# SyncE steps that a build-time planner holds back, and fifteen weight low parts moved to GpSimd

## The chip, the cores and the metric

The kernel runs on one core of a Trainium2 chip. The metric is the device time of one execution in microseconds (us); lower is better. One core has TensorE (PE in the profile: matmuls and transposes, reading its operands from SBUF and writing PSUM), VectorE (DVE), ScalarE (ACT), GpSimd (POOL) and SyncE (SP), which here only starts DMA transfers. Every engine executes its instructions in the order in which the program holds them, and SP and ACT each start their DMAs in that order too.

## What is computed

The reference is one transformer block over x of 2048 tokens by 640, in fp32: a pre-norm sliding-window attention with 32 heads of 20 and a window of 256 keys, an output projection and the residual, then a pre-norm GEGLU feed-forward with 1536 inner columns and a second residual.

```python
q, k, v = split(layernorm(x) @ wqkv)              # 32 heads of 20
scores = q @ k.T * 20 ** -0.5                     # key j visible to query i if 0 <= i - j < 256
h = x + softmax(masked scores) @ v @ wo
out = h + (gelu(layernorm(h) @ w_gate) * (layernorm(h) @ w_up)) @ w_down
```

## The kernel before

**Tiles.** The tokens are 16 blocks of 128; two blocks make a chunk (8 chunks of 256 tokens). The 640 columns are 5 slices of 128 (`KC` = 5). The feed-forward is cut in three column groups of 512 (`FG` = 3). A product in fp32 precision is made as three fp16 matmuls: each operand is split into a high part, its fp16 value, and a low part, the fp16 value of what is left, and hi·hi, hi·lo and lo·hi are added up in PSUM. So each weight matrix needs a high and a low part (`w3h` and `w3l` are those of the output projection wo; the tile `gu` holds those of the first gate and up groups).

**Weights.** The class `Weight` loads a matrix in 5 slices (128 x 640, or 128 x 512 for gate and up) through a ring `wsl` of three slots, once for the largest value and once more for the split. `split` makes the high part on ScalarE (scale, round to fp16) and then queues `low`, which makes the low part in one of two ways: VectorE reads the fp32 slice, scales it and subtracts the high part in one `scalar_tensor_tensor`; or, for the first `spread` slices, ScalarE scales the fp32 slice in place and GpSimd subtracts. Before, `SPREAD` is 0, and gate and up's first group gave no number: all their low parts are VectorE's. When the low part is done, the slot of the ring is free again.

**Attention.** For each block, `x_lane` loads x into `xt`, normalises it, makes its two fp16 parts (`xp`) and turns them with two DMA transposes, `xh<-xp` and `xl<-xp`. The products of a chunk for q and k go through ScalarE and VectorE to DRAM (`qk<-qks`, started on ACT's queue). The generator `stack` then brings them back in another layout: twelve loads on SP for each chunk, six `qT<-qk` and six `kT<-qk` of 160 KB each. It waits until q or k of the chunk is written, and until block 2c-3 has made its scores, since the new k overwrites keys in the ring `kT` that this block was the last to read. For each pair of heads of a block TensorE then makes scores in one form to find row maxima (`maxima`; VectorE reads them, `junk`), and in the other form for the exponents (`scores`; ScalarE's `pt<-rb,esc`), GpSimd masks the exponents in place (`pt<-pt`), and TensorE multiplies them with v (`pv<-pt,v`). The rows `rb` and `ra` are the two PSUM tiles for scores: the first `rb<-kT,qT` of a chunk is the first matmul that needs its loads. After the output projection VectorE adds the residual, which `residual` loads on SP (`ht<-in_x_dram`), and `wo_out` stores the sum on SP (`h_dram<-ht`).

**Feed-forward.** It starts near 500 us in the span, beside attention at first. Here `ht<-h_dram` brings the sums back, and weight sums (`ws`, `wsums`) are made on VectorE and GpSimd and exchanged through DRAM. The maxima `am` of later weights come from VectorE too.

**What sets the order.** The program is written by a planner, run when the kernel is built. Each piece of work is a generator that yields before each step the engines it needs (`self.engs`) and a function `self.need()`, the planner's time at which its operands will be there. The class `Clock` keeps a planned time for each engine from fixed durations. The main loop walks the lanes in order of rank; the first whose `Lane.start(now)` holds is stepped and writes its instructions. So the order within each queue is fixed at build time, and on the chip nothing passes an instruction ahead of it. Steps with TensorE among their engines have a rule of their own; for all others the last lines of `start` decide:

```python
return (all(nc.t[e] <= now + back for e in self.engs if e != "sync")
        and self.need() <= now + 0.1)
```

A step that only starts a DMA on SP has `self.engs == ("sync",)`: the first line is empty for it, and it is written as soon as the planned time is within 0.1 us of its operands' arrival. Where a DMA stands in SP's queue and its operands come later on the chip than planned, all behind it waits.

All device work goes through a recording helper, so nearly every row of the profile has its line, L199; the tile names tell the rows apart.

Of the kernel before, what the change touches and what calls it, by code (L numbers as in the profile page):

```python
# [24 lines left out]
KC = D // P  # L25
# [228 lines left out]
def block_kernel(ctx: ExitStack, tc: tile.TileContext, x, wqkv, wo, wg, wu, wd, out):  # L254
# [27 lines left out]
    def done(name):  # L282
# [12 lines left out]
    NW, AHEADQ = 3, 6  # L295
    SPREAD = 0
# [5 lines left out]
    FFBACK = dict(split_lane=0.4, scale_lane=0.4, chunk_lane=0.3, token_sums=0.1,  # L302
                  sums_lane=0.2, norm_lane=0.2)
    EARLY = 0.6
    PACE = 1.0
    SWAY = 4

# [12 lines left out]
    def on(eng, *reads, when=None, after=None):  # L320
        f = need(*reads, when=when, eng=eng)
        if after is not None:
            return (eng,), lambda: max(f(), nc.others(after, eng))
        return (eng,), f
# [214 lines left out]
    def products(n, term, ready=None, at_=None):  # L539


        ps = [at_[0]] if at_ else []
        col = at_[1] if at_ else 0

        def start(i):
            if ready and not ready(i) or not ps and opened["mm"] >= banks["mm"]:
                return INF
            t = nc.ready([x for ab in term(i) for x in ab], "tensor")
            return t if ps else max(t, nc.slot(psums["mm"], "mm", banks["mm"]))

        for i in range(n):
            yield ("tensor",), lambda i=i: start(i)
            if not ps:
                ps.append(bank("mm"))
            m = term(i)
            for k, (l, r) in enumerate(m):
                if k:
                    yield pe()
                o = ps[0][:, col:col + r.free_size()]
                nc.tensor.matmul(o, l, r, start=(i == 0 and k == 0),  # L560
                                 stop=(i == n - 1 and k == len(m) - 1))
                pos["dense"] += r.free_size() * 3 // len(m)
        return o
# [19 lines left out]
    wq = wqp.enter_context(tc.tile_pool(name="wq", bufs=1, side="right"))  # L583
    wp = attn.enter_context(tc.tile_pool(name="wp", bufs=1))
# [3 lines left out]
    gu = ffw.tile([P, 4 * KC * 512], F16, name="gu")  # L588
# [3 lines left out]
    gu = gu.rearrange("p (a c f) -> p a c f", c=KC, f=512)  # L592
# [174 lines left out]
    def stack(c, which, d):  # L767
# [10 lines left out]
        for par in range(2):  # L778
            for m, i in enumerate(((0, 0, 1), (0, 1, 0))[which]):
                rows = slice(64 * par + DH * m, 64 * par + DH * m + DH)  # L780
                if c > 1:
                    yield ("sync",), lambda: nc.moved["sync"] - PACE
                nc.sync.dma_start(to[rows], d.rearrange("(a d i) m n -> a m d i n", a=2,
# [652 lines left out]
    def split_lane():  # L1436
        for i, w in [(1, weights[1]), (0, weights[0]), *enumerate(weights)][:2] + list(
                enumerate(weights))[2:]:
            yield on("scalar", when=lambda: w.scaled)
            if i <= NW:  # L1440
                yield from w.split(wq if i < NW else wp, SPREAD)
                continue
            yield on("scalar", when=lambda: W["v"].ready)
            kind, fg = later[i - NW - 1]
            if fg == 0 and kind != "d":
                a = 2 * (kind == "u")
                yield from w.split((gu[:, a], gu[:, a + 1]))
                continue
            k = 1 if fg else 0
            yield on("scalar", when=lambda: ffpools[k])  # L1450
            yield from w.split(ffpools[k], 2)
# [106 lines left out]
    class Lane:  # L1558
# [11 lines left out]
        def start(self, now):  # L1570

            if "tensor" in self.engs:
                return nc.t["tensor"] <= now + AHEAD and self.need() <= max(now, nc.t["tensor"])
            name = self.gen.__name__
            back = self.back
            if name in ("split_lane", "scale_lane"):
                back = PREP if not W["o", 0].ready else FFPREP
            elif name == "x_lane":
                back = EARLY if not B[XF].full else LATE
            elif name == "max_out" and not W["v"].ready:  # L1580
                back = RAMPMAX
            if isinstance(self.engs, Soon):
                back = max(back, OUT)
            if ffpools[1]:
                back = FFBACK.get(name, OUT)
            return (all(nc.t[e] <= now + back for e in self.engs if e != "sync")
                    and self.need() <= now + 0.1)

    load_x(0)
    load_x(1)  # L1590
# [3 lines left out]
    for i, n in enumerate("qkv"):  # L1594
        W[n].load(rooms[n])
        W[n].room(wq)
        if i:
            load_x(i + 1)
    load_x(NR)
    lanes = [x_lane([0], "x"), x_lane([1], "xb"), x_lane([2], "xc"), x_lane([3], "xd"),  # L1600
             x_lane(range(NR, NB), "x"),
             split_lane(), *(scale_lane([i], str(i)) for i in range(NW)),
             scale_lane(range(NW, len(weights)), "0"), load_lane(), ones_lane(), big_lane(),
             first_norm_lane()]
# [6 lines left out]
    now = 0.0  # L1611
# [85 lines left out]
```

## Time and profile before

| | before |
|---|---|
| time, median of 3 runs | 1022.89 us (1022.6 to 1025.46) |
| the profiled execution, its own time | 1022.7 us |
| its span | 1020.8 us |
| TensorE clock granted, mean over the span | 0.998 |
| TensorE busy | 998.5 us (98%) |
| VectorE busy | 748.3 us (73%) |
| ScalarE busy | 437.9 us (43%) |
| GpSimd busy | 299.4 us (29%) |

The span runs from the first to the last instruction of the profiled execution; its own time holds 1.9 us more. A row of the busy table gives for an engine the time in which it worked, its share of the span and the number of instructions. A row of the waits gives the waiting engine and tile, what released it, and then the total in us, the number of times and the longest. A row of the timeline gives a start, a duration, engine, operation, the tile written `<-` the tiles read, a count where like rows are joined, and in brackets the idle time before it with its releaser. Rows with SPq show when SP started a DMA, not when it landed.

### The profile page before, as it was taken

The page shows a single profiled execution, that of the slowest core. Times are in us where ns is not written, and L with a number is a line of the kernel's source. Part 1 is how long each engine was busy: PE and PEld are TensorE (multiplying, and loading weights), DVE is VectorE, ACT ScalarE, POOL GpSimd, SP SyncE. Part 2 cuts the span into 40 slices and gives each one's busy share as a digit, 9 for nine tenths or more (in the row PEclk, how much of TensorE's full clock was granted, in tenths as well). Part 3 has the DMA queues.
Part 4 walks back from the last instruction along what each step waited for, and adds up shares of the span by engine and source line. Part 5 has one row for each costly group of instructions (what it writes and reads, how often), then busy time and mean ns, then how long its engine had stood idle before and what let it go on. Part 6 is the DMA issues. An engine that isn't in the chain of part 4 may idle for free.

```text
span 1020.8 us, 30772 instructions
## 1 busy us (share of the span) xinstructions
PE 998.5 (98%) x12925; PEld 698.8 (68%) x12925; DVE 748.3 (73%) x2221; ACT 437.9 (43%) x706; POOL 299.4 (29%) x489
## 2 busy tenths in 40 slices
PE   8999999998999999999999999989999999999998
PEld 7876677675776766776655664567777777777776
DVE  6888999885776757675688787798996975544553
ACT  6514645664445654555557643522222222221220
POOL 7102224343333432333335511254313300000000
PEclk9999999999999999999999999999999999999999
DMA  8658686271460723315303433233553532222211
GB/s 306 135 116 172 190 167 169 75 132 55 95 140 20 121 75 85 75 45 106 131 29 105 84 126 103 78 129 106 154 181 90 162 137 78 78 97 85 78 53 52
DMA packets 105835, 112.68 MB, mean 110 GB/s; under 512 B 38368, under 2 KB 79584, under 8 KB 105696
## 3 DMA queue, kind: packets, MB, share of 16 engines
q1 hardware_dynamic: 93600, 99.97, 36.4%
q10 hardware_dynamic: 12096, 10.75, 3.4%
q8 instruction: 101, 1.65, 0.7%
q14 instruction: 38, 0.31, 0.1%
HBM read 73.73 MB, written 28.84 MB: 100 GB/s over the span
## 4 chain that ended last, share of the span: by engine, by line
PE 83%; DMA 7%; DVE 5%; issue 2%; ACT 2%; SPq 1%; POOL 0%; DVEq 0%; ACTq 0%; POOLq 0%
PE mm L199 43%; PE pv L199 12%; PE ra L199 12%; PE rb L199 10%; PE tp L199 7%; DMA kT<-qk 3%; DMA qk<-qks 2%; DVE junk L199 1%; SPq L199 1%; DMA qT<-qk 1%; ACT pt L199 1%; DVE am L199 0%; DVE w1l L199 0%; DVE ht L199 0%; DMA wsl<-in_wo_dram 0%
## 5 line engine op out<-in xcount | busy, mean ns | idle before, releaser
L199 POOL TENSOR_SCALAR_AFFINE_SELECT pt<-pt 128x512 f32<-128x512 f32 x352 | 176.7, 518 | 277.5 <-ACT pt L199 261.4
L199 DVE CUSTOM_DVE_ANT_0 junk<-rb,band 128x320 bf16<-128x320 f32 x224 | 109.5, 489 | 48.5 <-PE rb L199 43.3
L199 DVE CUSTOM_DVE_ANT_0 junk<-ra,band 128x320 bf16<-128x320 f32 x224 | 109.4, 489 | 38.9 <-PE ra L199 33.4
L199 ACT ACTIVATE pt<-rb,esc 128x640 f32<-128x640 f32 (+2 forms) x129 | 98.3, 769 | 81.2 <-PE rb L199 65.5
L199 ACT ACTIVATE pt<-ra,esc 128x640 f32<-128x640 f32 (+2 forms) x127 | 96.6, 767 | 75.0 <-PE ra L199 63.9
L199 PE MATMUL pv<-pt,v 128*21 128x128 f32 x2880 | 105.3, 276 | 0.3 <-POOL pt L199 0.2
L199 PEld LDWEIGHTS <-ah 128*128 128x128 f16 x768 | 75.1, 98 | 28.4 <-issue 1.2
L199 ACT ACTIVATE gel<-gel,ffk 128x512 f32<-128x512 f32 x36 | 26.0, 722 | 144.0 <-DVE gel L199 144.0
L199 PEld LDWEIGHTS pv<-pt,v 128*21 128x21 f32 x2880 | 68.8, 100 | 10.8 <-issue 1.0
L199 PEld LDWEIGHTS <-ws 128*128 128x128 f16 x720 | 70.4, 98 | 8.2
L199 PEld LDWEIGHTS <-qT 60*64 60x64 f16 x1280 | 30.4, 104 | 66.4 <-issue 53.1
L199 PEld LDWEIGHTS <-kT 62*64 62x64 f16 x2880 | 63.5, 107 | 11.6 <-issue 8.0
L199 PEld LDWEIGHTS <-gu 128*128 128x128 f16 x440 | 42.0, 98 | 36.1 <-issue 1.7
L199 DVE SCALAR_TENSOR_TENSOR ht<-mm,ffk,ht 128x320 f32<-128x320 f32 x96 | 52.2, 545 | 12.0 <-PE mm L199 10.0
L199 ACT CAST ah<-gel 128x512 f16<-128x512 f32 x48 | 29.7, 618 | 66.7 <-DVE gel L199 64.7
L199 PE MATMUL mm<-xh,w1h 128*128 128x256 f16 x200 | 54.7, 274 | 0.9 <-DVE qks L199 0.9
L199 PE MATMUL mm<-xl,w1h 128*128 128x256 f16 x200 | 54.7, 273 | 0.0
L199 PE MATMUL mm<-xh,w1l 128*128 128x256 f16 x200 | 54.7, 273 | 0.0
L199 PE MATMUL rb<-kT,qT 60*64 60x320 f16 (+4 forms) x636 | 41.2, 283 | 9.5 <-DMA kT<-qk 8.8
L199 PE MATMUL mm<-w3h,oh 128*128 128x320 f16 x160 | 48.2, 301 | 0.0
L199 PE MATMUL mm<-w3l,oh 128*128 128x320 f16 x160 | 48.2, 301 | 0.0
L199 PE MATMUL mm<-w3h,ol 128*128 128x320 f16 x160 | 48.2, 301 | 0.0
(299 smaller groups left out, 2522.5 us busy)
## 6 DMA issues: line engine op xcount, KB each, us to landing
ws<-wsums SPq DMA_DIRECT2D x24, 640.0 KB
qk<-qks ACTq DMA_DIRECT2D x32, 256.0 KB
qT<-qk SPq DMA_DIRECT2D x48, 160.0 KB
kT<-qk SPq DMA_DIRECT2D x48, 160.0 KB
wsums<-ws SPq DMA_DIRECT2D x12, 640.0 KB
ht<-in_x_dram SPq DMA_DIRECT2D x16, 320.0 KB
h_dram<-ht SPq DMA_DIRECT2D x16, 320.0 KB
ht<-h_dram SPq DMA_DIRECT2D x16, 320.0 KB
```

Source lines behind the costliest of these rows:

```text
L199: r = real(*args, **kw)
```

## The change

Two rules of the planner change. First, a step that only starts a DMA on SP is written when its operands have, by the planner's clock, been there for 1 us (`HELD`), where before it could be written 0.1 us ahead of them. The loads of q and k (`stack`) and the weights' loads (`load_lane`) keep the old rule. Held are the stores `h_dram<-ht`, the residual's loads `ht<-in_x_dram`, the loads of x (`xt`), the turns `xh<-xp` and `xl<-xp`, and the feed-forward's exchanges through DRAM (`wsl` and `ht` from `h_dram`, the turns of h, `wsums` and `ws`). Second, all five low parts of wo and all five of each of the first gate and up groups take the second way: ScalarE scales the slice in place, GpSimd subtracts.

```diff
     EARLY = 0.6
+    HELD = 1.0
     PACE = 1.0
...
             if i <= NW:
-                yield from w.split(wq if i < NW else wp, SPREAD)
+                yield from w.split(wq if i < NW else wp, SPREAD if i < NW else KC)
                 continue
...
             if fg == 0 and kind != "d":
                 a = 2 * (kind == "u")
-                yield from w.split((gu[:, a], gu[:, a + 1]))
+                yield from w.split((gu[:, a], gu[:, a + 1]), KC)
                 continue
...
                 back = max(back, OUT)
             if ffpools[1]:
                 back = FFBACK.get(name, OUT)
+            late = 0.1 if self.engs != ("sync",) or name in ("stack", "load_lane") else -HELD
             return (all(nc.t[e] <= now + back for e in self.engs if e != "sync")
-                    and self.need() <= now + 0.1)
+                    and self.need() <= now + late)
```

Every matmul stays; SP has as many instructions as before. The order moves on all engines from about 84 us of the span on, and TensorE's is the same again from about 680 us. Three places are shown.

SP's queue around the loads of chunk 3, before (`qk_2547` and `qk_2930` are chunk 3's q and k in DRAM; the turns and loads of x among them belong to later blocks):

```order
L199 DMA qT<-qk_2547 20x16x256 x5
L199 DMA ht<-in_x_dram 128x640
L199 DMA_TRANSPOSE xh<-xp 128x5x128
L199 DMA_TRANSPOSE xl<-xp 128x5x128
L199 DMA xt<-in_x_dram 128x640
L199 DMA qT<-qk_2547 20x16x256
L199 DMA kT<-qk_2930 20x16x256 x5
L199 DMA_TRANSPOSE xh<-xp 128x5x128
L199 DMA_TRANSPOSE xl<-xp 128x5x128
L199 DMA xt<-in_x_dram 128x640
L199 DMA kT<-qk_2930 20x16x256
```

The same place of the change, where the same data are called `qk_2566` and `qk_3073`:

```order
L199 DMA ht<-in_x_dram 128x640
L199 DMA qT<-qk_2566 20x16x256 x6
L199 DMA kT<-qk_3073 20x16x256 x6
L199 DMA h_dram<-ht 128x640
L199 DMA ht<-in_x_dram 128x640
L199 DMA_TRANSPOSE xh<-xp 128x5x128
```

The twelve loads now follow each other; the four turns and two loads of x that stood among them stand elsewhere.

SP's queue around the loads of chunks 6 and 7, the last two, before:

```order
L199 DMA qT<-qk_7165 20x16x256 x6
L199 DMA kT<-qk_7788 20x16x256 x6
L199 DMA h_dram<-ht 128x640
L199 DMA ht<-in_x_dram 128x640
L199 DMA h_dram<-ht 128x640
L199 DMA qT<-qk_8927 20x16x256 x3
L199 DMA ht<-in_x_dram 128x640
L199 DMA qT<-qk_8927 20x16x256 x3
L199 DMA kT<-qk_9349 20x16x256 x6
```

And in the change:

```order
L199 DMA qT<-qk_7585 20x16x256 x6
L199 DMA kT<-qk_7946 20x16x256 x3
L199 DMA h_dram<-ht 128x640
L199 DMA kT<-qk_7946 20x16x256 x3
L199 DMA ht<-in_x_dram 128x640
L199 DMA h_dram<-ht 128x640
L199 DMA ht<-in_x_dram 128x640
L199 DMA h_dram<-ht 128x640
L199 DMA ht<-in_x_dram 128x640
L199 DMA qT<-qk_9219 20x16x256 x6
L199 DMA kT<-qk_9903 20x16x256 x3
L199 DMA h_dram<-ht 128x640
```

In both chunks a store of a residual sum now stands between the third and the fourth load of k; the last three loads of chunk 7 follow behind the last row shown.

GpSimd's queue at the first gate and up weights, in the change (`AFFINE_SELECT pt<-pt` are the masks, `gu<-wsl,gu` the subtractions; the rows `lyx` and `lyh` belong to layer norms):

```order
L199 TENSOR_TENSOR lyh<-lveh,mhalf 128x1
L199 TENSOR_TENSOR gu<-wsl,gu 128x512 x2
L199 AFFINE_SELECT pt<-pt 128x4x64 x2
L199 AFFINE_SELECT pt<-pt 128x4x128
L199 TENSOR_TENSOR gu<-wsl,gu 128x512
L199 AFFINE_SELECT pt<-pt 128x4x64 x2
L199 AFFINE_SELECT pt<-pt 128x4x128
L199 TENSOR_TENSOR gu<-wsl,gu 128x512
```

Before, only masks and rows of layer norms stood here: subtractions of 512 or 640 columns now stand between the masks of one pair of heads and the next, one or two at a time.

## The prediction, made before the changed kernel had run

> **What bounds the kernel now.** I read the busy table first, then TensorE's waits, then the places in the timeline where the long waits end, then who was late there.
>
> ```profile
> PE 998.5 (98%) x12925; PEld 698.8 (68%) x12925; DVE 748.3 (73%) x2221; ACT 437.9 (43%) x706; POOL 299.4 (29%) x489
> ...
> PE rb L199 <- DMA kT<-qk: 8.8, 4, 4.7
> ...
> PE tp L199 <- DVE am L199: 1.9, 1, 1.9
> ...
> PE mm L199 <- DVE ht L199: 0.4, 1, 0.4
> ...
> PE pv L199 <- POOL pt L199: 0.2, 1, 0.2
> ```
>
> TensorE works in 998.5 of 1020.8 us. The change leaves its matmuls as they are, so it can win only out of the 22.3 us in which TensorE stands, and the rest of its waits are small or lie ahead of the first row that moves. The largest is one thing: four times, 8.8 us in all, the first scores of a chunk wait for the loads of k. The other candidate is VectorE in the feed-forward, 1.9 and 0.4 us. GpSimd's masks are waited for once, 0.2 us.
>
> The longest wait, 4.7 us, is chunk 3's. SP's timeline ahead of it, then a step of the chain of waits (start, duration, what ran), then the matmul:
>
> ```profile
> 214.25 11.19 SPq L199 DMA_DIRECT2D kT<-qk  x5
> 230.35 1.30 SPq L199 DMA_TRANSPOSE xh<-xp  x1
> ...
> 233.66 0.77 SPq L199 DMA_DIRECT2D kT<-qk  x1
> ...
> 233.66 3.91 DMA kT<-qk
> ...
> 237.61 0.32 PE L199 MATMUL rb<-kT,qT 60*64 60x64 f16 x3 [4.71 <-DMA kT<-qk]
> ```
>
> Eleven loads had been started by 225.44 (214.25 + 11.19). The twelfth stood behind two turns whose operands were not there before 230.35, and behind a load of x; it started at 233.66, landed 3.9 us later, and TensorE went on at once. SP's order made this wait, not the transfers. Chunks 5 and 7 show milder forms:
>
> ```profile
> 346.43 1.53 SPq L199 DMA_TRANSPOSE xh<-xp  x1
> ...
> 366.76 0.33 PE L199 MATMUL rb<-kT,qT 60*64 60x320 f16 x3 [1.62 <-DMA kT<-qk]
> ...
> 463.93 2.35 SPq L199 DMA_DIRECT2D qT<-qk  x3
> 466.39 0.45 SPq L199 DMA_DIRECT2D ht<-in_x_dram  x1
> ...
> 469.31 8.87 SPq L199 DMA_DIRECT2D kT<-qk  x6
> ...
> 484.61 0.33 PE L199 MATMUL rb<-kT,qT 60*64 60x320 f16 x3 [2.24 <-DMA kT<-qk]
> ```
>
> In chunk 5 turns stand among the loads, in chunk 7 a residual's load, with a store ahead. With 4.71, 1.62 and 2.24 us, some 0.2 us of the 8.8 are left for the fourth. Chunk 6 had its twelve loads in one piece, and no wait:
>
> ```profile
> 398.36 4.72 SPq L199 DMA_DIRECT2D qT<-qk  x6
> 403.13 7.94 SPq L199 DMA_DIRECT2D kT<-qk  x6
> ```
>
> The wait at 237 has a second price, the granted clock behind it:
>
> ```profile
> 220.00:240.00 20.00, 15.29 (x265) 10.46 (x255) 10.22 (x36) 8.88 (x15) 7.28 (x16) 0.94 0.45 109
> 240.00:260.00 20.00, 20.00 (x436) 13.73 (x435) 15.83 (x59) 11.81 (x19) 8.29 (x17) 0.97 0.11 36
> ...
> 242.19 0.30 PE L199 MATMUL mm<-w2h,xl 128*128 128x320 f16 x1
> 242.33 0.30 PE L199 MATMUL mm<-w2h,xh 128*128 128x320 f16 x1
> ```
>
> The column after the busy times is the clock: 0.94 and 0.97 over 20 us each, (0.06 + 0.03) x 20 = 1.8 us. The last two rows show the distance of two matmuls at full clock, 0.14 us.
>
> **The loads of q and k.** First I ask how long twelve loads need. Chunk 6's last started by 411.07; with 3.91 us to land that is 411.07 + 3.91 - 398.36 = 16.6 us. Chunk 7's, with another load among them, took 484.61 - 463.93 = 20.7 us. Then how long they have: from the last scores of block 2c-3, which free the ring, to the first matmul that needs them. I counted TensorE's work between the two in the order of both kernels, each pair of neighbouring forms at its mean distance of starts in the trace; for before this gives the traced distances to 0.9 us. A pair of heads, for example, costs what these rows' starts show, 1.2 us:
>
> ```profile
> 242.69 0.33 PE L199 MATMUL rb<-kT,qT 60*64 60x256 f16 x8
> 242.86 0.31 PE L199 MATMUL ra<-qT,kT 62*64 62x128 f16 x12
> 243.10 0.85 PE L199 MATMUL pv<-pt,v 128*21 128x128 f32 x24
> 243.89 0.31 PE L199 MATMUL mm<-w2h,xl 128*128 128x320 f16 x1
> ```
>
> The distances (estimates) for chunks 3 to 7 go from 28.8, 29.0, 29.7, 27.6, 21.9 to 22.5, 23.9, 23.2, 22.0, 28.6 us. So the planner, with held steps out of the way, also asks for the scores some 5 us sooner in four chunks, and that spends the slack. All are still above 20.7. Hence **-8.8** for the waits and **-1.8** for the clock, less what comes back:
>
> - Chunk 3 has its loads in one piece: 22.5 against 16.6. A DMA also waits for an earlier one on the ring of eight that SP and ACT share, here a store of q that is released 11.1 us ahead of the scores and needs about as much with the load behind it: 0.3.
> - Chunk 4 keeps a store, a turn and a load of x ahead of its loads and a residual's load among them: 23.9 against 20.7 and a turn of 1.3 us more: 0.5, for a turn that is late.
> - Chunks 5 and 6: 0. In chunk 6 a store stands between the third and fourth load of k, but its product ends some 15 us ahead of the scores, and three loads need about 3 x 1.3 + 3.9 = 7.8 us (7.94 / 6 = 1.3 each to start).
> - Chunk 7: the last part of k is now made 14.8 us ahead of the scores, where before it was 28.0. Behind it come two halves on ScalarE and VectorE (0.8, from the groups below at half their width), its store to DRAM, and the three loads of 7.8 us. The store's time, from the chain of waits:
>
> ```profile
> 285.46 4.46 DMA qk<-qks
> ...
> 354.79 6.99 DMA qk<-qks
> ```
>
>  That is 13.1 to 15.6 us against 14.8: 0.3.
>
> Together **+1.1**. The bounds: 0, and, if each of chunks 3 to 6 lost once more the 4.1 us that lie between 16.6 and 20.7, (24.8 x 4) - (22.5 + 23.9 + 23.2 + 22.0) = 7.6.
>
> **The low parts.** What the fifteen cost on VectorE now, and what like ones cost on ScalarE and GpSimd (groups of instructions: count | busy, mean ns | idle before), and the stage in which they lie:
>
> ```profile
> L199 DVE SCALAR_TENSOR_TENSOR w3l<-wsl,sw,w3h 128x640 f16<-128x640 f32 x5 | 4.5, 911 | 0.0
> L199 DVE SCALAR_TENSOR_TENSOR gu<-wsl,sw,gu 128x512 f16<-128x512 f32 x10 | 8.5, 862 | 0.2 <-ACT gu L199 0.2
> ...
> L199 POOL TENSOR_TENSOR w12l<-wst,w12h 128x640 f16<-128x640 f32 x2 | 3.7, 1835 | 3.2 <-ACT wst L199 3.2
> L199 POOL TENSOR_TENSOR w5l<-wst,w5h 128x512 f16<-128x512 f32 x2 | 2.3, 1159 | 7.6 <-ACT wst L199 7.6
> ...
> L199 ACT ACTIVATE wst<-wst,sw 128x512 f32<-128x512 f32 x8 | 5.8, 722 | 0.4
> L199 ACT ACTIVATE wst<-wst,sw 128x640 f32<-128x640 f32 x6 | 5.0, 829 | 0.3
> ...
> 80.00:200.00 120.00, 118.14 (x1867) 82.91 (x1859) 109.76 (x382) 69.46 (x123) 37.38 (x65) 1.00 0.64 158
> ```
>
> VectorE gives up 4.5 + 8.5 = 13.0 us. ScalarE takes 5 x 0.83 + 10 x 0.72 = 11.4 us and is busy 69.5 of 120 us there: 0, hidden in its idle half. GpSimd takes 5 x 1.84 + 10 x 1.16 = 20.8 us beside 37.4 busy. VectorE is the fullest helper of the stage (109.8 of 120), but TensorE stands only 120 - 118.14 = 1.9 us in it, so 13 us less on VectorE are worth between 0 and -1.9; I take **0**, as those gaps stand against no low part.
>
> What a subtraction can delay is a mask behind it. ScalarE hands each pair of heads to GpSimd:
>
> ```profile
> 239.09 1.49 POOL L199 TENSOR_SCALAR_AFFINE_SELECT pt<-pt 128x256 f32<-128x256 f32 x3 [5.96 <-ACT pt L199]
> ```
>
> A pair's masks take 1.5 us, after GpSimd had idled 6. In the changed order TensorE has 3.9 to 5.6 us of work between a pair's last scores and its first product with v. An exponent of about 0.8, masks of 1.5 and one subtraction of 1.2 to 1.8 make 3.5 to 4.1 us: it fits, or nearly. Where two subtractions stand together 4.7 do not always fit. I take **+0.5**; bounds 0, and 15 x 1.0 us if every one shows.
>
> **The feed-forward.** TensorE's waits there for `am` and `ht` (1.9 + 0.4) stand in a stretch where VectorE is behind. In the new order the transposes that wait for `am` stand 24 matmuls later, at 0.14 us each 3.4 us, more than the 1.9. But the stretch is reordered as well and VectorE still is behind there: I take **-1.0**, bounds 0 and -2.3.
>
> **The sum** against the profiled span: 1020.8 - 8.8 - 1.8 + 1.1 + 0.5 - 1.0 = 1010.8. The execution's own time has 1.9 us more: 1012.7. The median of the runs is 0.2 above the profiled one: **1012.9, say 1013**.
>
> **A rule on the port.** The trace shows GpSimd and VectorE slowing each other. In the ramp, two low parts on VectorE beside a GpSimd subtraction, and two like ones just after:
>
> ```profile
> 19.18 3.35 POOL L199 TENSOR_TENSOR xl<-gu,xh 128x640 f16<-128x640 f32 x2
> 20.38 2.83 DVE L199 SCALAR_TENSOR_TENSOR w1l<-gu,sw,w1h 128x640 f16<-128x640 f32 x2 [0.38 <-ACT w1h L199]
> ...
> 23.93 1.66 DVE L199 SCALAR_TENSOR_TENSOR w1l<-gu,sw,w1h 128x640 f16<-128x640 f32 x2
> ```
>
> 1.41 us each beside GpSimd, 0.83 alone. If VectorE were slowed so in all 20.8 us of subtractions, it would lose 20.8 x (1 - 0.83/1.41) = 8.6 us of the 13.0 it gains. That is rival D. The Trainium skill has the rule (GPSIMD Engine Reference, section Specifications): GpSimd's way into SBUF is shared with VectorE, and contends with VectorE's instructions that have two SBUF inputs; the trace agrees with 1.41 against 0.83.
>
> **Rivals.**
>
> - **A, stores still in the way** (chunks 6 and 7): the two stores that now stand among the loads of k are late as the turns were, and each chunk waits the 2.2 us of chunk 7 now. 1012.9 + 4.4 - 0.3 = 1017.0. For it: the excerpt of SP's queue, and chunk 7's 14.8 us. Against: the store waits on a product that ends well ahead.
> - **B, the slack is spent**: the scores come 5 us sooner and the loads need 25 us, so the removed 8.8 us come back over four chunks. 1012.9 - 1.1 + 8.8 = 1020.6, no change. For it: chunk 6 has 22.0 where chunk 7 needed 20.7 now. Against: clean loads take 16.6.
> - **D, the port**: VectorE's lost 8.6 us show in full: 1021.5, no change. Against: most of VectorE's work here reads PSUM, and 13.0 were freed.
> - **C, slower: subtractions ahead of masks.** Each of the fifteen delays the masks queued behind it on GpSimd, these the products with v, and with PSUM full TensorE stands; at 1.0 us each, 1012.9 - 0.5 + 15 = 1027.4. The gain is gone from 0.5 us each, slower starts at 0.9. For it: GpSimd runs in order and a subtraction takes as long as a pair's slack. Against: TensorE waited for a mask once, 0.2 us, and 3.9 us is the least distance.
>
> **How the numbers follow.** A measurement of this kernel tells changes from about 0.3%, 3.1 us, so same is 1019.8 to 1026.0. Chances: forecast 0.62, A 0.12, B 0.08, D 0.04, C 0.14. Faster is forecast and A, 0.74; same B and D, 0.12; slower 0.14. The forecast's own range is 1009 (nothing comes back, -1.1, the masks cost nothing, -0.5, the feed-forward gives all, -1.3, and a little of the 1.9) to 1017 (one chunk loses the 4.1). To hold 8 in 10 it has to take in A, B and D: 1009 to 1022.
>
> **What would show it.** Right: TensorE's wait for `kT` under 2 us in all; the clock at 1.00 from 220 to 260 us; SP's twelve loads of chunk 3 in one piece; VectorE 13 us less busy, GpSimd 21 and ScalarE 11 more; waits of `pv` for `pt` under 1 us. Wrong: waits of 2 us before the first scores of chunks 4, 6 or 7 (A, B), TensorE waiting for VectorE between 90 and 200 us (D), or for `pt` there (C).

## The result, and the profile after

The change made the kernel faster: 1017.74 us, median of six runs (1014.38 to 1019.55), against 1022.75 us for the kernel before in six runs beside it (1021.04 to 1025.46). The ratio of the runs is 0.9927, with a 95% interval of 0.9904 to 0.9950; the two medians alone give less, 0.9951, and the means of the six runs 0.9941. The profiled execution took 1018.26 us, its span is 1016.5 us, 4.3 us shorter than before's.

First the busy table of the profile after, and TensorE's longest waits in it:

```profile
PE 998.2 (98%) x12925; PEld 699.3 (69%) x12925; DVE 749.2 (74%) x2206; ACT 446.6 (44%) x721; POOL 313.2 (31%) x504
```

```profile
PE ra L199 <- DVE mxs L199: 1.9, 2, 1.4
PE tp L199 <- DVE ht L199: 1.6, 1, 1.6
PE pv L199 <- issue: 1.1, 1, 1.1
PE mm L199 <- DVE ht L199: 1.0, 1, 1.0
...
PE tp L199 <- DVE ws L199: 0.8, 1, 0.8
PE tp L199 <- DVE am L199: 0.6, 1, 0.6
...
PE ra L199 <- DMA kT<-qk: 0.3, 1, 0.3
```

The 8.8 us of waits for k are gone: the 0.3 us that are left stand at 53 us, in an early chunk and ahead of all that the change moved. New are waits for VectorE: 1.9 us for row maxima (`mxs`) and 1.6 us for the normalised `ht`. `<- issue` means that the profile shows nothing that TensorE waited for; there are 2.1 us of it (1.1 here, and 0.6 and 0.4 in the rows left out), against 0.3 before. VectorE, which gave up 13.0 us of low parts, is not less busy: 749.2 against 748.3 us. GpSimd is 13.8 us busier and ScalarE 8.7.

TensorE's idle time by stage is the width of a stretch less the first busy time behind it. Before:

```profile
200.00:300.00 100.00, 94.71 (x1871) 66.50 (x1870) 75.45 (x281) 52.50 (x83) 38.09 (x78) 0.98 0.52 106
300.00:400.00 100.00, 98.17 (x1879) 68.93 (x1876) 68.38 (x250) 55.28 (x84) 38.00 (x80) 1.00 0.32 70
400.00:500.00 100.00, 97.76 (x1966) 68.35 (x1968) 65.96 (x251) 52.91 (x81) 35.52 (x75) 1.00 0.36 80
...
600.00:700.00 100.00, 97.34 (x578) 56.68 (x577) 83.39 (x187) 37.82 (x57) 30.98 (x24) 1.00 0.29 102
```

And after:

```profile
80.00:200.00 120.00, 115.59 (x1827) 80.58 (x1824) 103.97 (x372) 78.07 (x137) 51.84 (x78) 1.00 0.67 162
...
200.00:300.00 100.00, 97.66 (x1963) 69.59 (x1962) 80.01 (x285) 55.57 (x86) 40.38 (x84) 1.00 0.42 102
300.00:400.00 100.00, 99.83 (x1917) 70.00 (x1916) 74.17 (x271) 57.40 (x89) 39.01 (x83) 1.00 0.34 78
400.00:500.00 100.00, 99.91 (x1974) 69.78 (x1974) 64.35 (x238) 51.66 (x79) 34.05 (x72) 1.00 0.37 96
...
600.00:700.00 100.00, 97.53 (x583) 57.10 (x582) 83.38 (x186) 38.87 (x59) 33.38 (x27) 1.00 0.28 99
```

From 200 to 500 us, where the loads of chunks 3 to 7 lie, idle time falls from 9.4 to 2.6 us, and the clock of 200 to 300 us goes from 0.98 to 1.00. From 80 to 200 us, where the low parts are made, it rises from 1.9 (the row for that stretch is in the prediction) to 4.4. In the feed-forward it is 2.7 and 2.5.

Chunk 3's loads on SP, after: they stand in one piece, and the last of the six of k is started only at 227.67 (within the second row).

```profile
208.59 5.37 SPq L199 DMA_DIRECT2D qT<-qk  x6
214.00 14.42 SPq L199 DMA_DIRECT2D kT<-qk  x6
```

Where the 1.6 us wait comes from is seen at 148 to 152 us, in the timelines of VectorE, GpSimd and TensorE after:

```profile
148.20 1.11 DVE L199 SCALAR_TENSOR_TENSOR lyah<-lyh,lveh 128x1 f32<-128x1 f32 x1
...
150.13 1.59 DVE L199 TENSOR_SCALAR ht<-ht,lmvh,lyh 128x640 f32<-128x640 f32 x1
...
148.13 1.16 POOL L199 TENSOR_TENSOR gu<-wsl,gu 128x512 f16<-128x512 f32 x1
150.22 1.15 POOL L199 TENSOR_TENSOR gu<-wsl,gu 128x512 f16<-128x512 f32 x1 [0.93 <-ACT wsl L199]
...
151.78 0.66 PE L199 MATMUL tp<-ident,ht 128*128 128x128 f32 x4 [1.63 <-DVE ht L199]
```

A step of one element for each partition (`lyah`) lasts 1.11 us, and ends when GpSimd's subtraction does (149.3). The normalisation of `ht` behind it lasts 1.59 us and ends some 0.3 us after the next subtraction. TensorE's transposes wait for it.

The 1.9 us for `mxs` have another cause. The longest piece, 1.4 us, ends at 170.96 us, and on VectorE two rows ahead of those maxima had stood for late slices of weights, the first for 1.50 us:

```profile
167.85 0.69 DVE L199 TENSOR_REDUCE am<-wsl 128x1 f32<-128x512 f32 x1 [1.50 <-DMA wsl<-in_wu_dram]
```

### The profile page after: what moved, and what is told of

Read it like the earlier page. It is cut to its first block, busy times and chain, and to the rows that moved or that the text cites. A ratio compares the mean times of both kernels' runs of the same rounds, so it can differ in the third digit from the quotient of the medians.

```text
span 1016.5 us, 30774 instructions
## 1 busy us (share of the span) xinstructions
PE 998.2 (98%) x12925; PEld 699.3 (69%) x12925; DVE 749.2 (74%) x2206; ACT 446.6 (44%) x721; POOL 313.2 (31%) x504
## 4 chain that ended last, share of the span: by engine, by line
PE 82%; DVE 7%; DMA 5%; ACT 3%; POOL 2%; issue 2%; SPq 0%; ACTq 0%; DVEq 0%; POOLq 0%
PE mm L199 41%; PE ra L199 12%; PE pv L199 11%; PE rb L199 10%; PE tp L199 7%; DVE junk L199 1%; DMA wsl<-in_wu_dram 1%; DMA kT<-qk 1%; DMA qk<-qks 1%; POOL pt L199 1%; DVE am L199 1%; DMA qT<-in_wqkv_dram 1%; ACT pt L199 1%; DVE ht L199 1%; POOL gu L199 0%
## 5 line engine op out<-in xcount | busy, mean ns | idle before, releaser
L199 POOL TENSOR_SCALAR_AFFINE_SELECT pt<-pt 128x512 f32<-128x512 f32 x352 | 174.4, 511 | 300.8 <-ACT pt L199 284.9
L199 DVE CUSTOM_DVE_ANT_0 junk<-ra,band 128x320 bf16<-128x320 f32 x238 | 116.4, 489 | 50.5 <-PE ra L199 45.1
L199 ACT ACTIVATE pt<-rb,esc 128x640 f32<-128x640 f32 (+2 forms) x135 | 102.4, 765 | 81.6 <-PE rb L199 61.1
L199 DVE CUSTOM_DVE_ANT_0 junk<-rb,band 128x320 bf16<-128x320 f32 x210 | 102.8, 489 | 35.0 <-PE rb L199 29.7
L199 ACT ACTIVATE pt<-ra,esc 128x640 f32<-128x640 f32 (+2 forms) x121 | 92.2, 769 | 67.3 <-PE ra L199 59.1
L199 POOL TENSOR_TENSOR gelt<-gelt 128x256 f32<-128x256 f32 x18 | 15.5, 859 | 112.6 <-ACT gelt L199 112.6
L199 PE MATMUL mm<-w2h,xl 128*128 128x320 f16 x160 | 48.1, 300 | 0.0
```

Source lines behind the costliest of these rows:

```text
L199: r = real(*args, **kw)
```

## The experiments

Most kernels keep the planner's decisions of before or of the change, and alter only what is written into the queues. So TensorE's order is that of their parent, instruction for instruction, and one thing differs. Only `held_only` and `lows_only` have an order of TensorE of their own, since there the planner decides anew, and `pull_held` has that of `held_only`. Runs of one kernel scatter by 4 to 10 us; where a term is smaller than that, the profile's waits decide, not the time. TensorE's waits are given from the one profiled execution of each kernel, which need not be a typical one: that of `held_only` is the slowest of its eight runs (1022.53 us), that of `pull_held` the second slowest of twelve (1025.74 us), that of `pull_before` the second fastest of twelve (1015.63 us).

**The hold alone**, the low parts on VectorE as before:

```diff
-                yield from w.split(wq if i < NW else wp, SPREAD if i < NW else KC)
+                yield from w.split(wq if i < NW else wp, SPREAD)
...
-                yield from w.split((gu[:, a], gu[:, a + 1]), KC)
+                yield from w.split((gu[:, a], gu[:, a + 1]))
```

> The held SP steps alone; the fifteen low parts stay on VectorE. Theory P (the hold removes the waits for k, the moved subtractions give back about 2 us between 80 and 200 us by holding VectorE up): TensorE's wait for kT falls from 8.8 us to 1 to 4 (one piece of turns stands among chunk 3's last loads in this order), no 1.6 us wait for ht near 150 us, time 1014 to 1018. Theory Q (the new order of the helpers costs the 2 us, whoever makes the low parts; VectorE needs the relief): the same kT wait, but TensorE waits 3 us or more for VectorE between 80 and 200 us, time 1019 to 1022.

Measured: 1020.0 us, ratio to before 0.9954 (0.9935 to 0.9974). Its waits:

```profile
PE rb L199 <- DMA kT<-qk: 2.7, 2, 2.0
...
PE ra L199 <- DMA qk<-qks: 2.3, 1, 2.3
...
PE rb L199 <- DMA qT<-mT: 1.4, 1, 1.4
```

The wait for k fell to 3.1 us with 0.4 for `ra`, as both theories had it, and the wait of 1.6 us for `ht` isn't there. But the time is in theory Q's range, not in P's, while theory Q's waits for VectorE between 80 and 200 us aren't there either. This order has waits of its own, 2.3 us for a store of q or k and 1.4 for the transposed maxima, and its clock stays low: the 2.0 us wait for k near 228 us comes with a granted clock of 0.91 from 220 to 240 us, the 2.3 us near 357 us with 0.93 and 0.98 from 340 to 380 us. Over its eight runs the mean clock is 0.997, where the change has 1.000. A planner that decides anew makes new small waits, and the hold alone gives only part of the gain.

**The low parts alone**, SP's rule as before:

```diff
-            late = 0.1 if self.engs != ("sync",) or name in ("stack", "load_lane") else -HELD
+            late = 0.1 if self.engs != ("sync",) or name in ("stack", "load_lane") else 0.1
```

> The fifteen low parts on GpSimd alone; SP's steps at the old rule. Theory P: turns and loads of x still stand among the loads of k (chunk 4 here), kT wait 4 to 9 us, plus 1 to 2 us of waits for VectorE held up by subtractions: 1021 to 1026. Theory Q: VectorE's relief is worth some us by itself: 1015 to 1019.

Measured: 1023.05 us, 0.9992 (0.9973 to 1.0011), no difference from before. Its waits:

```profile
PE ra L199 <- DMA kT<-qk: 4.1, 3, 3.3
PE mm L199 <- DVE qks L199: 2.5, 2, 1.7
...
PE tp L199 <- DVE ht L199: 1.4, 1, 1.4
```

Turns stand among chunk 4's loads here, and 3.3 us of wait for k go with them; VectorE is waited for as theory P said. The second half of the change brings nothing by itself.

**SP's order alone.** Before's order, but at the first load of a six all six are started (chunks 3 to 7), while the planner goes on as before:

```diff
+                if c > 2 and not (par or m):
+                    for p2 in range(2):
+                        for m2, i2 in enumerate(((0, 0, 1), (0, 1, 0))[which]):
+                            r2 = slice(64 * p2 + DH * m2, 64 * p2 + DH * m2 + DH)
+                            nc.nc.sync.dma_start(
+                                to[r2], d.rearrange("(a d i) m n -> a m d i n", a=2, d=DH)[p2, i2])
```

> The order of before on all engines, except that on SP the six loads of q, and the six of k, of chunks 3 to 7 follow each other, so that no turn or load of x, residual load or store stands inside a six; nothing else is moved, and the low parts stay on VectorE. Theory P (SP's order makes the wait for k): chunk 3's 4.7 us wait goes, and with it the 0.94 and 0.97 of granted clock; kT wait 8.8 to 2 to 4 us, since chunk 7 has its store and residual load ahead as before; time 1015 to 1019 and TensorE's other waits as before. Rival (the loads come late because of the DMA engines or the ring, not because of what stands between them): kT wait still 6 us or more, 1021 or more.

Measured: 1017.93 us, 0.9943 (0.9924 to 0.9962); its profiled span is 1013.8 us. The wait for k, and the window that held the slow clock:

```profile
PE rb L199 <- DMA kT<-qk: 2.3, 2, 1.5
```

```profile
220.00:260.00 40.00, 38.66 (x817) 26.96 (x813) 30.00 (x110) 23.00 (x37) 17.10 (x35) 1.00 0.32 68
```

Some loads of SP's queue stand earlier and nothing else moves, and the time falls by 0.57%. Chunk 3's wait is gone, and the 2.3 us left are chunk 5's (1.5) and chunk 7's (0.7); `issue` has 2.0 us near 217 and 225 us. It shows that SP's order made the wait for k and the slow clock. It is as large, within the intervals, as the whole change.

**The low parts in before's order.** The planner books VectorE; the queues get ScalarE's scaling and GpSimd's subtraction:

```diff
-                nc.vector.scalar_tensor_tensor(lo, w, sc, hi, op0=ALU.mult, op1=ALU.subtract)
+                nc.nc.scalar.activation(w, w, AF.Copy, scale=sc)
+                nc.nc.gpsimd.tensor_tensor(lo, w, hi, op=ALU.subtract)
```

> The order of before exactly, except that the fifteen low parts are made by ScalarE (scaling in place) and GpSimd (subtraction) where VectorE made them. Theory P (GpSimd's subtractions hold VectorE up and give back what the relief brings): TensorE's busy time from 80 to 200 us within 1.5 of before's 118.1, kT wait still 7 to 10, time 1021 to 1024. If the relief of VectorE is worth something by itself: 1019 or less. If the masks wait behind the subtractions (rival C): waits of pv for pt of 3 us or more between 80 and 200 us, over 1025.

Measured: 1028.05 us, 1.0035 (1.0017 to 1.0052), slower. Its waits and its stage from 80 to 200 us:

```profile
PE rb L199 <- DMA kT<-qk: 7.1, 4, 4.9
...
PE pv L199 <- POOL pt L199: 1.3, 2, 1.1
```

```profile
80.00:200.00 120.00, 114.66 (x1778) 80.31 (x1777) 95.36 (x350) 76.39 (x135) 51.20 (x77) 0.99 0.61 159
```

VectorE is 14.4 us less busy in the stage than before (109.76), and TensorE works 3.5 us less. No theory fits: rival C's time came (over 1025), but masks are waited for 1.3 us, not 3. The rest of the loss in the stage is spread: the waits for row maxima grow from 0.3 to 1.1 us, those for ScalarE's exponents, which can now stand behind its scaling, from 0.8 to 1.7. The clock is lower too, 0.91 from 100 to 120 us, where before had 1.00. So the run shows the net of relief and cost, a loss of 4 us in an order that wasn't made for the move; the relief by itself it doesn't show.

**The low parts in the change's order, back on VectorE.** The planner books ScalarE and GpSimd; VectorE makes the part at the same place:

```diff
-                nc.scalar.activation(w, w, AF.Copy, scale=sc)
...
-                nc.gpsimd.tensor_tensor(lo, w, hi, op=ALU.subtract)
+                nc.nc.vector.scalar_tensor_tensor(lo, w, sc, hi, op0=ALU.mult,
+                                                  op1=ALU.subtract)
```

> The order of the change on TensorE and SP exactly, and on the others but for the fifteen low parts, which VectorE makes at the place where ScalarE and GpSimd made them (no scaling on ScalarE, no subtraction on GpSimd). Theory P: the small steps and the normalisation of ht on VectorE are short again (lyah 0.2 instead of 1.1 us, ht 0.6 instead of 1.6 us near 148 to 152 us), the 1.6 us wait of tp for ht is gone; TensorE's busy time from 80 to 200 us rises from 115.6 by 1.5 or more, time 1014 to 1017. Theory Q: the waits stay or grow with 13 us more on VectorE: 1018 to 1022.

Measured: 1019.16 us, 0.9958 (0.9944 to 0.9973), with this at the top of its waits from 80 to 200 us:

```profile
PE ra L199 <- DVE mxs L199: 3.2, 5, 0.8
...
PE tp L199 <- DVE ht L199: 0.4, 1, 0.4
```

The wait for `ht` went from 1.6 to 0.4 us, as theory P had it, but those for maxima grew from 1.9 to 3.2, in five small pieces: TensorE works 114.2 us in the stage, less than the change's 115.6. That, and the time, speak for theory Q: in this order VectorE needs the relief. To see how much, it ran again beside the change:

> The change's order with the fifteen low parts on VectorE, again, beside the change on one chip. If the move to GpSimd is worth something in this order: 1 to 3 us above the change, with waits of ra for mxs of 3 us or more. If it is worth nothing: within 1 us of it.

> The change itself once more, on one chip with the next two, and for the scatter from run to run. Both theories: 1016 to 1019, 0.5 to 0.9% under before. Its profile shows which of the single waits of the first one come back: the waits of tp for ht (1.6 us) and of ra for mxs (1.9) between 80 and 200 us should, since they follow from the order; the waits that the profile puts down to nothing (2.1 us in all, at 227, 284 and 291 us) need not.

Measured: 1018.72 us, 0.9951 (0.9934 to 0.9968), against 1015.83 us, 0.9925 (0.9901 to 0.9949) for the change. The medians are 2.9 us apart, and its profile has 3.1 us of waits of `ra` for `mxs`, both as expected if the move is worth something. The intervals overlap, but all eleven of its runs lie above five of the change's six. I take some 2 to 3 us for the move in this order; the size isn't settled. The change itself came out just below the 1016 to 1019 expected. Its second profile has a span of 1012.4 us, 4.1 less than its first. Its waits:

```profile
PE tp L199 <- DVE ht L199: 1.6, 1, 1.6
...
PE ra L199 <- DMA kT<-qk: 1.0, 1, 1.0
...
PE ra L199 <- DVE mxs L199: 0.4, 1, 0.4
```

The wait for `ht` came back to the tenth, so it belongs to the order. That for `mxs` shrank from 1.9 to 0.4 (a slice of weights was 0.54 us late, not 1.50), and the 2.1 us of `issue` are gone: these came and went within one program. Idle time from 80 to 200 us was 3.0 us this time, against 4.4 in the first profile and before's 1.9:

```profile
80.00:200.00 120.00, 117.02 (x1855) 82.04 (x1854) 105.66 (x378) 78.36 (x138) 53.44 (x81) 1.00 0.66 161
```

**Smaller pieces.** The change's order, each subtraction in pieces of 128 columns:

```diff
-                nc.gpsimd.tensor_tensor(lo, w, hi, op=ALU.subtract)
+                    for k in range(0, self.shape[1], P):
+                        s = slice(k, k + P)
+                        nc.nc.gpsimd.tensor_tensor(lo[:, s], w[:, s], hi[:, s], op=ALU.subtract)
```

> The order of the change exactly; each of the fifteen subtractions is written as pieces of 128 columns (4 or 5 GpSimd instructions). Theory P, with VectorE held for the whole of a GpSimd instruction: the longest hold falls from about 1.1 to about 0.4 us, the wait for ht near 150 us falls from 1.6 to under 0.8 us, time 0.5 to 1.5 us less than the change. If VectorE is slowed by the sum of GpSimd's work, in whatever pieces: no difference, within 0.5 us of the change.

Measured: 1016.22 us, 0.9925 (0.9903 to 0.9946). The same place, VectorE, GpSimd, TensorE:

```profile
147.61 0.37 DVE L199 SCALAR_TENSOR_TENSOR lyah<-lyh,lveh 128x1 f32<-128x1 f32 x1
...
148.09 0.61 DVE L199 TENSOR_SCALAR xt<-xt,lmvx,lyx 128x640 f32<-128x640 f32 x1
...
149.04 0.68 DVE L199 TENSOR_SCALAR ht<-ht,lmvh,lyh 128x640 f32<-128x640 f32 x1
...
147.54 1.84 POOL L456 TENSOR_TENSOR gu<-wsl,gu 128x128 f16<-128x128 f32 x4
...
149.78 0.66 PE L199 MATMUL tp<-ident,ht 128*128 128x128 f32 x4 [0.22 <-DVE ht L199]
```

GpSimd needs longer for the part, 1.84 us in four pieces against 1.16 in one, and yet VectorE's steps are shorter: `lyah`, which runs beside the pieces, takes 0.37 against 1.11 us. The normalisation of `xt`, as wide as that of `ht`, lies wholly beside the pieces and takes 0.61 us, no more than in the change, where no subtraction runs beside it. So what holds a step of VectorE is the one GpSimd instruction that it meets, not the sum of GpSimd's work. The 0.68 us of `ht`, against 1.59, prove less, since `ht` fell mostly into the gap between two subtractions (149.38 to 149.62). The wait fell from 1.6 to 0.2 us. The time can't be told from the change's.

**Twice the subtraction**, in the change's order, with the second like the first:

```diff
                 nc.gpsimd.tensor_tensor(lo, w, hi, op=ALU.subtract)
+                if self.sliced:
+                    nc.nc.gpsimd.tensor_tensor(lo, w, hi, op=ALU.subtract)
```

> The order of the change exactly, with each of the fifteen subtractions made twice on GpSimd, 18.8 us more of its work. If masks behind subtractions are near their limit (rival C): waits of pv for pt of 2 us or more appear, time 3 us or more above the change. If only VectorE is held up: TensorE's waits for ht and mxs between 80 and 200 us grow from 3.5 to 5 to 8 us and pv waits for pt stay under 1 us: 1 to 4 us above the change.

Measured: 1028.06 us, 1.0039 (1.0020 to 1.0058). Its waits, and GpSimd in front of the longest one for a mask:

```profile
PE tp L199 <- DVE ht L199: 3.7, 2, 3.4
PE pv L199 <- POOL pt L199: 3.2, 3, 2.0
```

```profile
201.67 1.16 POOL L452 TENSOR_TENSOR gu<-wsl,gu 128x512 f16<-128x512 f32 x1
202.77 1.49 POOL L199 TENSOR_SCALAR_AFFINE_SELECT pt<-pt 128x256 f32<-128x256 f32 x3
```

Both ways of loss appear, VectorE held up and masks behind subtractions. 18.8 us more of subtractions cost some 11 us (1.0039 - 0.9927 = 1.1% of 1023). Ahead of these masks stand four subtractions in place of two, 2.3 us more, and TensorE waits 2.0 us: the mechanism of rival C was there, with its limit less than one subtraction away from this order. About half of the 11 us is the clock, which in the stage from 80 to 200 us is 0.97, where the change has 1.00:

```profile
80.00:200.00 120.00, 112.19 (x1739) 77.28 (x1737) 100.97 (x346) 74.60 (x130) 61.53 (x83) 0.97 0.65 153
```

In the 20 us each from 100, from 140 and from 200 us it is 0.91, and 1.00 between: 3 x 0.09 x 20 = 5.4 us. The longest waits for `ht` (3.4 us) and for a mask (2.0) lie in the last two of these.

**Stores out of the loads**, in the order and pieces of `order_split`, with the edit of `pull_before`:

> The order of the change, subtractions in pieces of 128 columns, and the loads of q and of k of chunks 3 to 7 in sixes without a store or residual load among them. If stores among the loads of k still cost (rival A): kT wait 0 and 1 to 4 us less than with the pieces alone (1016.2). Theory P: chunks 6 and 7 were on time already, chunk 4's 1.4 us wait falls a little as a residual's load moves by three loads: within 1 us of it, 1015 to 1016.5.

Measured: 1018.02 us, 0.9936 (0.9911 to 0.9960), not to be told from the pieces alone. Chunk 4's wait for k, 1.4 us with the pieces alone, is gone, and 0.2 us in chunk 3 is all that is left from 84 us on (another 1.1 us stands at 53 us). There are 4.2 us of `issue` (0.9 in a row left out):

```profile
PE ra L199 <- issue: 1.9, 1, 1.9
PE rb L199 <- issue: 1.4, 1, 1.4
```

The stores among the loads of chunks 6 and 7 cost nothing that can be seen: no profile of the change's order has a wait of 0.2 us or more for them there, with or without this edit, unless GpSimd's work is doubled (0.2 us). Rival A falls.

**The hold and the sixes**, low parts on VectorE (`held_only` with the edit of `pull_before`):

> SP steps held, low parts on VectorE, and the loads of q and of k of chunks 3 to 7 in sixes. If the time hangs on SP's order alone: kT wait under 1.5 us, against 3.1 with the hold alone, and 1015 to 1018, as with before's order and the sixes (1017.9). If the new order that the hold gives costs something by itself (waits for a store of q or k near 357 us, for am near 673 us): 1018 to 1021.

Measured: 1021.44 us, 0.9985 (0.9964 to 1.0005). That is above both theories' ranges. The wait for k fell to 1.0 us as expected (0.6 in chunk 4, 0.4 ahead of 84 us), and another took its place. SP, ScalarE and TensorE at chunk 3:

```profile
208.53 7.83 SPq L789 DMA_DIRECT2D kT<-qk  x6
216.48 2.58 SPq L199 DMA_TRANSPOSE xh<-xp  x1
225.25 2.23 SPq L199 DMA_TRANSPOSE xl<-xp  x1
...
228.76 0.72 ACT L199 CAST xp<-xt 128x640 f16<-128x640 f32 x1 [5.99 <-DMA xl<-xp]
229.39 0.58 ACT L199 COPY oT<-pv 128x512 f32<-128x512 f32 x1
...
230.02 1.04 PE L199 MATMUL tp<-ident,oT 117*128 117x117 f32 x4 [4.39 <-ACT oT L199]
```

The loads now stand ahead of the turns, and SP stands 6.1 us more ahead of the second turn, by the profile for a store of q or k (`qk<-qks`). ScalarE has its next cast into `xp` written ahead of a copy that TensorE needs, the cast must wait until the turn has read `xp`, and so TensorE waits 4.4 us for the copy. The clock from 220 to 240 us is 0.83 with it, another 0.17 x 20 = 3.4 us. Putting loads first isn't free: the turn that is put behind them has a reader with a due time of its own. This is one execution, 4.3 us slower than the median; how much of the median this wait makes isn't shown.

## Why the prediction was right, and where it was off

The direction, the main mechanism and the wide range (1009 to 1022) held; the size was off. I had 10.0 us. The medians give 5.0, and the ratio 0.73% of 1023 us, 7.5 us, with an interval of 5 to 10; the second six runs of the change give 7.7 by their medians. With 1017.74 the median lies 0.7 us above the range that I gave the forecast by itself, and next to rival A's 1017.0, but A's sign, waits in chunks 6 and 7, is absent: the number is near A's by chance.

- **The loads of q and k** (-8.8 -1.8 +1.1). Right. In chunks 3 to 7 the wait for k is 0 in one profile of the change and 0.3 us in the other (chunk 4), against the 1.1 that I left standing; the 0.3 and 1.0 us of `ra` stand at 53 us. The clock from 200 to 300 us is 1.00. `pull_before` shows that SP's order made wait and clock. The clock was worth more than the 1.8 us that before's profile showed, for that execution was a good one: over the 22 runs of before beside the change's second six its mean is 0.9965, over those six 0.9997, and 0.0032 of 1020 us are 3.3 us (an estimate, as if all of the time went with the clock). Chunks 6 and 7, with their stores among the loads, were on time, and rival B, the spent slack, didn't come.
- **The low parts** (0 for VectorE, +0.5 for the masks). The mechanism failed here. The masks weren't waited for, but in both profiles TensorE waits 1.6 us for `ht`, because VectorE is held up. I had worked out what subtractions take from VectorE, 8.6 us, and set it against the 13.0 that it gains. That is a balance of busy time; what counts is the single step that meets a subtraction, on a chain with TensorE at its end. `order_split` shows this mechanism. So rival D was at work inside the forecast, at a fifth of its price. The sign "VectorE 13 us less busy" failed with it: from 80 to 200 us VectorE is 5.8 and 4.1 us less busy in the two profiles, so some 7 to 9 us of the 13.0 came back there (an estimate, since the stretch doesn't hold quite the same work), near the 8.6, but only 1.6 of them reached TensorE. GpSimd's bill was 18.8 us, not 20.8: a subtraction of 640 columns took 1.40 us, not the 1.84 of the row that I had taken it from.
- **The relief of VectorE**, which I took as 0, doesn't make up for its cost in before's order (`before_pool`, 0.35% slower), and in the change's the move is worth some 2 to 3 us (`order_vec`). That the planner had laid that order out with VectorE free is the likely reason, and isn't shown.
- **The feed-forward** (-1.0) was mis-sized: nothing came, 2.7 us of idle time against 2.5. The wait for `am` went from 1.9 to 0.6 us, as the 24 matmuls between should have it, but waits for `ht` and `ws` (1.0 and 0.8) took its place, with VectorE behind throughout the stretch.
- **Rival C** had 0.14. At 1.2 to 1.4 us for a subtraction it stayed off. `order_double` shows how near it was, and `before_pool` shows it beginning, 1.3 us, in another order.
- **Chance within one program** wasn't in my sum. The change's two profiles are 4.1 us apart; 2.1 us of `issue` and 1.5 of `mxs` in the first are most of that. The second execution took 1014.1 us, 1.4 more than my sum for the profiled one (1012.7).

With what belongs to the order in both profiles, +1.6 for `ht` in place of the +0.5 and 0 for the feed-forward, my sum for the span would have been 1010.8 + 1.1 + 1.0 = 1012.9, near the second profile's 1012.4. That is fitted afterwards, and to the faster of the two profiles.

## What to carry to other kernels

Where loads wait in a queue behind transfers whose data come late, the order of that one queue can be worth as much as all else, as it was here; look for the row that blocks, and give the moved row's own reader a look before it is put behind (4.4 us in `pull_held`). Work that is moved to a less busy engine is not paid in busy time: ask which small steps on a chain to TensorE it will meet, and keep its instructions short. A relief can be worth something in one order and less than its cost in another, so move the work in both orders before crediting it. And read the clock beside each wait, over all runs and not in the profile alone: here it made up to half of a difference in time.

## What the runs showed of the hardware

GpSimd can hold a step of VectorE for a whole instruction: a step of 0.2 us on one element for each partition took 1.11 us beside a subtraction of 1.16 us, and 0.37 us beside the same work in four pieces (0.2 us is what this step took in `order_vec`, where GpSimd has no subtraction there). The Trainium skill has this (SBUF — State Buffer, section SBUF: two separate sides): the pair of ports that the two share is locked by whichever starts first for its whole instruction, where VectorE's has two inputs in SBUF, as this one, or works in a mode of two ports. The pieces agree with a lock for the whole instruction, and not with a share of bandwidth. That it goes to the one that starts first isn't shown: by the profile the `ht` of the change starts at 150.13 us, the subtraction beside it at 150.22, and it is `ht` that is held.

With some waits of TensorE of about 2 us the granted clock falls, at a price of about as much again. The 2.0 us near 228 us in `held_only` came with a mean of 0.91 over 20 us, a price of 0.09 x 20 = 1.8 us, and so did the 2.0 us near 203 us in `order_double`; the 2.24 us near 484 us and the 1.62 near 367 in before came with 1.00. What decides it isn't shown.

TensorE stood up to 1.9 us for nothing that the profile names, at the last of a group of like matmuls or in the middle of one; the same program ran without it another time. The profile counts 101 transfers of instructions. In `pull_split` the stall that ends at 283.6 us follows one that landed at 282.0, some 10 us after the one before it, where from 80 to 500 us they come at a median distance of 6.7 us. Distances as long, up to 15 us near 99 us, also stand without a stall. That TensorE waits for its instructions there is a guess, and wasn't tried.
